# An attention and expert kernel on one core: more products of ones at the start, and two groups of loads issued by ScalarE

## The chip, the cores and the metric

The kernel runs on one core of one Trainium2 chip. The metric is the device time of the whole kernel in microseconds (us), the median of several executions. The engines are named as in the profile: PE (TensorE, products), PEld (its weight loads), DVE (VectorE), ACT (ScalarE), POOL (GpSimd) and SP (SyncE, which here only issues transfers). Each engine carries out its instructions in the order of its own queue; between engines they wait on semaphores. A transfer (DMA) is issued by SP or ACT, which each have a queue of their own (SPq, ACTq), and is carried out by 16 DMA engines; the issuing instruction itself takes time on the engine that issues it.

## The reference

Attention over two batches of eight heads, 576 positions of 64 values, in which each row keeps only its 32 largest scores; then a layer of four experts, weighted by probabilities that are divided by their sum.

```python
scores = scale * np.matmul(q, k.transpose(0, 1, 3, 2))
kth = np.partition(scores, -top_k, axis=-1)[..., -top_k:-top_k + 1]
scores = np.where(scores >= kth, scores, -1000000000.0)
attn = softmax(scores)                       # rows of 576
x = np.matmul(attn, v)                       # to (1152, 512)
p = domain_probs / (domain_probs.sum(-1, keepdims=True) + 1e-09)
for e in range(4):
    out += p[:, e:e + 1] * (np.maximum(x @ w1[e], 0.0) @ w2[e])
```

All inputs are 32-bit floats; w1 is 4 x 512 x 1024, w2 is 4 x 1024 x 512.

## The kernel before

The 1152 rows are cut into ten tiles: for each batch one of 64 rows and four of 128. The first tile worked on is the 64-row tile of batch 0. A tile is cut into units: a head for the tiles of 128 rows; for a tile of 64 rows a pair of heads, one in the upper and one in the lower half of the partitions. For each unit TensorE makes the scores, VectorE finds the 32 largest of each row (four times MAX8, line L666, with MATCH_REPLACE8, L668 and L670, between them), ScalarE takes the exponential, VectorE or ScalarE with GpSimd mask it (L717), and TensorE multiplies with the values. The expert layer of a tile (L894 to L896, L941) follows once its attention is done. 32-bit operands are split into a high and a low 16-bit part for this; only the first tile's attention works on 32-bit operands directly.

The order on every engine is written out by hand: pieces of work are given a place in one list (`at`, with the table `ISSUE`), and each engine's queue is filled in the order of that list. Code that stands outside `at` is put in where it stands, ahead of the list.

What happens at the start, and the names that matter:

- `kraw` holds the 576 keys of the eight heads of batch 0: `kraw0[:, 0:4, x, z, :]` the first 512 keys of head 4z+x, `kraw0[0:64, 4, ...]` the last 64 keys. `load_k0` (L1014 to L1016) issues two loads of 128 KB for one x; `load_k0_end` (L1022 to L1025) issues the two loads of the last 64 keys of all heads, 64 KB each.
- ACT issues `load_k0` for x = 0 and 2 (L1018, L1020). SP issues the queries of the first tile (`qraw`, two loads, L359), the last 64 keys, `load_k0` for x = 1 and 3, the queries of the second tile (`qraw`, L366), then four loads of the probabilities (`pn`, `norm_probs`, L1047 to L1050), and after those the first expert weights (`w`, L351) and the values (`vraw`, L334, L337).
- On TensorE a loop (L1039) multiplies a block of ones with itself into a bank that nobody reads. Then come the transposes of the first queries (L568, copied by ACT at L572), the transposes of the keys for x = 0 (L589, copied by ACT at L582 for the first 512 keys and at L583 for the last 64), and the scores of the first unit (L608, eight products). The first MAX8 (L666) reads these scores.
- `kv_gram` (L1070) sums squares over all of `kraw`; its diagonal goes to DVE at L1076 and a total back to it at L1079, L289.
- `norm_probs2` (L1053 to L1056) divides the probabilities by their sums on DVE; it is the first reader of the loaded `pn`. It stands in DVE's queue inside the first unit's search for maxima.
- ACT's table of functions is loaded (ACT_TABLE_LOAD) ahead of its first ACTIVATE (L1041), right behind ACT's own issues of loads. L382 squares the second tile's queries.

A queue of transfers uses eight semaphores in turn (`DMAHW0` to `DMAHW7` in the order below): an issue waits until the earlier transfer that raises the same semaphore has landed.

Of the kernel before, what the change touches and what calls it, by code (L numbers as in the profile page):

```python
# [229 lines left out]
def attn_moe_kernel(tc, q, k, v, probs, w1, w2, out):  # L230
    nc = tc.nc
    PE, ACT, DVE, POOL, SP = nc.tensor, nc.scalar, nc.vector, nc.gpsimd, nc.sync
# [38 lines left out]
    def at(place, fn, *args):  # L271

        i = len(known)
        known.append(fn.__name__)
        heapq.heappush(events, (ISSUE[i][0] if ISSUE else place, i, 0, fn, args))

    def bank(p, tag):
        return p.tile([128, 512], F32, tag=tag, name=tag)
# [17 lines left out]
    with tc.manual_schedule(engines={getattr(mybir.EngineType, x) for x in MANUAL}):  # L296
# [10 lines left out]
        pn = cp.tile([128, 10, E], F32, name="pn")  # L307
# [16 lines left out]
        kraw0 = scratch.tile([128, 5, 4, 2, D], F32, name="kraw0")  # L324
# [30 lines left out]
        def load_q(t, eng=SP):  # L355
            r = rawp.tile([128, 8, D], F32, tag="raw", name="qraw")
            if t == tiles[0]:
                for z in range(2):
                    eng.dma_start(out=r[0:64].rearrange("p (x z) d -> p x z d", z=2)[:, :, z, :],  # L359
                                  in_=q[t[0], 4 * z:4 * z + 4, t[1]:t[1] + 64, :].rearrange("h p d -> p h d"))  # L360
            elif t[2] == 64:
                for z in range(2):
                    eng.dma_start(out=r[z * 64:(z + 1) * 64, 0:4, :],
                                 in_=q[t[0], 4 * z:4 * z + 4, t[1]:t[1] + 64, :].rearrange("h p d -> p h d"))
            else:
                eng.dma_start(out=r, in_=q[t[0], :, t[1]:t[1] + 128, :].rearrange("h p d -> p h d"))  # L366
            qraw[t] = r
# [646 lines left out]
        def load_k0(eng, x):  # L1014
            for z in range(2):
                eng.dma_start(out=kraw0[:, 0:4, x, z, :], in_=k[0, 4 * z + x, 0:512, :].rearrange("(p j) d -> p j d", j=4))  # L1016

        load_k0(ACT, 0)  # L1018
        load_q(tiles[0])
        load_k0(ACT, 2)  # L1020

        def load_k0_end():  # L1022
            for z in range(2):
                SP.dma_start(out=kraw0[0:64, 4, :, z, :],
                             in_=k[0, 4 * z:4 * z + 4, 512:576, :].rearrange("h p d -> p h d"))  # L1025

        at(-200, load_k0_end)
        at(-199, load_k0, SP, 1)
        at(-198, load_k0, SP, 3)

# [5 lines left out]
        DVE.memset(ones, 1.0)  # L1036
        DVE.memset(kraw0[64:128, 4], 0.0)
        warm = bank(ps_m2, "m2")
        for _ in range(24):  # L1039
            PE.matmul(warm[:, 0:128], lhsT=ones.bitcast(BF16)[:, 0:128], rhs=ones.bitcast(BF16)[:, 0:128], start=True, stop=True)  # L1040
        ACT.activation(stp.tile([128, 1], F32, tag="warm", name="warm"), ones[:, 0:1], AF.Exp)  # L1041
        DVE.memset(pn, 1.0)
# [3 lines left out]

        def norm_probs():  # L1047
            for g, r0, n, m in ((0, 0, 128, 4), (4, 512, 64, 1), (5, S, 128, 4), (9, S + 512, 64, 1)):
                SP.dma_start(out=pn[0:n, g:g + m, :],
                             in_=probs[r0:r0 + n * m, :].rearrange("(t p) e -> p t e", p=n))  # L1050

        def norm_probs2():
# [73 lines left out]
        def norm_x0():  # L1126
            POOL.tensor_scalar(pn[:, 0:5], pn[:, 0:5], ix[:, 0:1], None, op0=OP.mult)

        at(P["probs"], norm_probs)
        at(P["probs2"], norm_probs2)  # L1130
        at(P["probs2"] + 1, norm_x0)
# [78 lines left out]
        for m, (e, j) in enumerate(worder):  # L1210
            for a in (0, 2):
                n = 4 * m + a
# [4 lines left out]
            g = P["gram"][m]  # L1217
            w_scale(e, j, g)
            g = max(P["split"][m], g + P["diag"], raw_used.get((e, j), 0) + 0.1)
# [5 lines left out]
        while events:  # L1225
            place, i, n, f, args = heapq.heappop(events)
# [38 lines left out]
```

## Time and profile before

| | us |
|---|---|
| median of 3 runs | 538.57 |
| lowest, highest run | 537.21, 541.6 |
| profiled execution | 536.48 |
| its span, from the first to the last instruction | 534.7 |
| mean granted TensorE clock | 0.979 of full |

How to read it: an engine's busy time is a mean over stages with different limits, so what matters is which engine the chain of work that ended last runs through at a given time. That chain is followed back from the last instruction; at each step it goes to whatever released the instruction, or to the one before it on its engine. "issue" is time in which nothing that the profile shows was waited for. The granted clock of TensorE has two levels here, 1.2 GHz (0.50 of full) and 2.4 GHz (1.00); a mean in between is a stretch that holds both. Before the first record the column shows 1.00.

### The profile page before, as it was taken

To read this page: it belongs to the slowest core of one execution; us is meant where nothing else is said; L and a number is where in the kernel's file an instruction comes from. 1 tells how busy PE (TensorE), PEld (TensorE's weight loads), DVE (VectorE), ACT (ScalarE), POOL (GpSimd) and SP (SyncE) were. 2 spreads that over 40 slices of the span, in tenths; PEclk is the share of its full clock that TensorE was granted. 3 is DMA by queue.
4 is the path that set the end of the run, shared out by engine and by line. 5 is a ranking of instruction groups with operands and counts; after the bars stand their busy time and mean duration, and the time that the engine had idled before them with its cause. 6 is when DMAs were issued, how large, how long until landed. Compare 5 with 4: busy or idle time off the path is not lost.

```text
span 534.7 us, 16328 instructions
## 1 busy us (share of the span) xinstructions
PE 502.9 (94%) x6738; PEld 382.4 (72%) x6738; DVE 433.2 (81%) x966; ACT 366.8 (69%) x610; POOL 361.1 (68%) x395
## 2 busy tenths in 40 slices
PE   7887677789999999999999999999999999999996
PEld 5566664676777777777877688678777876777766
DVE  3999999999999999999999998998889895500102
ACT  3999999998668788788768667676466664252112
POOL 0489999999776777786957867586556664434211
PEclk8998899899999999999999999999999999999999
DMA  7999999544743547384635642542532222302001
GB/s 172 350 328 296 268 252 220 107 71 86 104 83 75 101 86 128 95 145 84 134 78 97 120 90 66 73 79 47 75 72 54 51 56 50 60 22 46 12 2 32
DMA packets 142780, 58.37 MB, mean 109 GB/s; under 512 B 130097, under 2 KB 134449, under 8 KB 142705
## 3 DMA queue, kind: packets, MB, share of 16 engines
q1 hardware_dynamic: 139280, 54.50, 48.7%
q10 hardware_dynamic: 3424, 2.82, 1.7%
q8 instruction: 53, 0.87, 0.7%
q14 instruction: 23, 0.18, 0.1%
HBM read 25.45 MB, written 2.36 MB: 52 GB/s over the span
## 4 chain that ended last, share of the span: by engine, by line
PE 78%; DVE 17%; ACT 2%; issue 1%; DMA 1%; SPq 0%; DVEq 0%; ACTq 0%
PE m L941 33%; PE m L894 11%; PE m L896 11%; PE m L895 11%; DVE m L666 7%; PE av L777 5%; PE ps L653 5%; DVE w L670 4%; DVE w L668 2%; DVE w L717 2%; DMA kraw<-in_k_dram 1%; PE m L952 1%; ACT w L542 1%; PE av L952 0%; PE ps L649 0%
## 5 line engine op out<-in xcount | busy, mean ns | idle before, releaser
L896 PE MATMUL m<-xt,w 128*128 128x128 f16 (+1 forms) x1280 | 199.8, 215 | 1.4 <-POOL w L545 1.4
L941 PE MATMUL m<-w,h 128*128 128x512 f16 (+1 forms) x912 | 191.8, 383 | 0.0
L894 PE MATMUL m<-xt,w 128*128 128x128 f16 (+1 forms) x1120 | 179.1, 215 | 0.0
L895 PE MATMUL m<-xt,w 128*128 128x128 f16 (+1 forms) x1120 | 179.0, 215 | 0.0
L666 DVE MAX8 m<-w 128x8 f32<-128x576 f32 x216 | 161.6, 755 | 3.0
L941 PEld LDWEIGHTS <-h 128*128 128x128 f16 (+1 forms) x912 | 81.7, 101 | 89.0 <-issue 3.1
L896 PEld LDWEIGHTS <-w 128*128 128x128 f16 x1280 | 124.1, 99 | 1.5 <-POOL w L545 1.5
L894 PEld LDWEIGHTS <-w 128*128 128x128 f16 x1120 | 108.9, 99 | 3.0 <-issue 1.0
L895 PEld LDWEIGHTS <-w 128*128 128x128 f16 x1120 | 108.6, 99 | 1.9
L670 DVE MATCH_REPLACE8 w<-m,w 128x576 f32<-128x576 f32 x144 | 106.9, 742 | 0.0
L919 POOL TENSOR_TENSOR h<-hf,h 128x512 f16<-128x512 f32 x56 | 64.9, 1158 | 56.1 <-ACT hf L912 48.7
L738 POOL TENSOR_TENSOR a<-w,a 128x512 f16<-128x512 f32 x68 | 78.8, 1160 | 22.7 <-ACT a L736 13.0
L727 POOL TENSOR_TENSOR w<-w,d 128x576 f32<-128x576 f32 x49 | 62.7, 1280 | 37.0 <-ACT d L724 36.8
L710 ACT ACTIVATE w<-ps,nb,es 128x576 f32<-128x576 f32 x68 | 56.2, 827 | 42.9 <-DVE m L666 35.1
L905 ACT ACTIVATE h<-m 128x512 f16<-128x512 f32 x72 | 42.5, 590 | 57.2 <-PE m L896 39.3
L666 DVE MAX8 m<-ps 128x8 f32<-128x576 f32 x72 | 54.4, 756 | 19.6 <-PE ps L608 7.1
L988 DVE SCALAR_TENSOR_TENSOR o<-m,pniw,o 128x512 f32<-128x512 f32 (+1 forms) x13 | 9.7, 746 | 56.2 <-PE m L941 46.7
L736 ACT ACTIVATE a<-w 128x576 f16<-128x576 f32 x68 | 45.9, 679 | 11.8 <-POOL w L727 9.3
L668 DVE MATCH_REPLACE8 w<-m,ps 128x576 f32<-128x576 f32 x72 | 53.8, 747 | 0.0
L653 PE MATMUL ps<-kt,qa 128*128 128x288 f16 x128 | 34.3, 288 | 14.5 <-DVE w L717 13.7
L777 PEld LDWEIGHTS <-at 128*128 128x128 f16 (+1 forms) x1008 | 37.0, 100 | 7.5 <-DMA at<-a 2.2
L777 PE MATMUL av<-vt,at 128*128 128x65 f16 (+1 forms) x1008 | 40.1, 195 | 1.3 <-DMA at<-a 1.3
(163 smaller groups left out, 784.0 us busy)
## 6 DMA issues: line engine op xcount, KB each, us to landing
w<-in_moe_w_dram SPq DMA_DIRECT2D x16, 1024.0 KB, 7.2
qraw<-in_q_dram SPq DMA_DIRECT2D x8, 256.0 KB, 3.5
qb<-qa SPq DMA_DIRECT2D x16, 128.0 KB, 2.6
out_dram<-o ACTq DMA_DIRECT2D x8, 256.0 KB, 2.0
at<-a SPq DMA_TRANSPOSE x68, 3.3
vraw<-in_v_dram SPq DMA_DIRECT2D x2, 512.0 KB, 9.1
nraw<-in_v_dram SPq DMA_DIRECT2D x4, 256.0 KB, 3.4
kraw<-in_k_dram SPq DMA_DIRECT2D x4, 256.0 KB, 3.3
```

What stands on the lines that cost most here:

```text
L653: PE.matmul(ps[:, 0:288], lhsT=src[:, x, :], rhs=kt[x].rearrange("p c n -> p (c n)")[:, ks], start=(j == 0), stop=(j == 1))
L666: DVE.max(m, s_t[u] if r == 0 else w_t[u])
L668: DVE.match_replace(rows2(w_t[u]), m, s_t[u], NEG)
L670: DVE.match_replace(w_t[u], m, w_t[u], NEG)
L727: POOL.tensor_tensor(w, w, g, op=OP.mult)
L738: POOL.tensor_tensor(a[:, 640:1152], w[:, 0:512], a[:, 0:512], op=OP.subtract)
L777: PE.matmul(o, lhsT=att[:, blk, ps], rhs=r, start=(i == 0), stop=(i == len(seq) - 1))
L894: PE.matmul(o, lhsT=HI[e, 0, c][:, fc], rhs=xs(0, c), start=(c == 0), stop=False)
L895: PE.matmul(o, lhsT=HI[e, 0, c][:, fc], rhs=xs(1, c), start=False, stop=False)
L896: PE.matmul(o, lhsT=LO[e, 0, c][:, fc], rhs=xs(0, c), start=False, stop=(c == 3))
L919: POOL.tensor_tensor(h[:, 1], hf, h[:, 0], op=OP.subtract)
L941: PE.matmul(y[z * 64:z * 64 + M, :], lhsT=h_t[es, qd][:, p // 2, h0:h0 + M], rhs=w, start=(fc == 0 and p == 0), stop=(fc == 7 and p == 2))
```

## The change

Three edits at the start of the program; nothing else is changed, and the order of the instructions on DVE and POOL is the same.

1. The loop over products of ones runs 36 times instead of 24.
2. The two loads of the last 64 keys are split up: the one for heads 4 to 7 (z = 1) is issued by ACT, between `load_k0` for x = 0 and for x = 2; the one for heads 0 to 3 (z = 0) stays on SP.
3. The four loads of the probabilities are issued by ACT instead of SP.

```diff
+        def load_k0_end(eng, z):
+            eng.dma_start(out=kraw0[0:64, 4, :, z, :],
+                          in_=k[0, 4 * z:4 * z + 4, 512:576, :].rearrange("h p d -> p h d"))
+
         load_k0(ACT, 0)
         load_q(tiles[0])
+        load_k0_end(ACT, 1)
         load_k0(ACT, 2)
-
-        def load_k0_end():
-            for z in range(2):
-                SP.dma_start(out=kraw0[0:64, 4, :, z, :],
-                             in_=k[0, 4 * z:4 * z + 4, 512:576, :].rearrange("h p d -> p h d"))
-
-        at(-200, load_k0_end)
+        at(-200, load_k0_end, SP, 0)
         at(-199, load_k0, SP, 1)
         at(-198, load_k0, SP, 3)
...
-        for _ in range(24):
+        for _ in range(36):
             PE.matmul(warm[:, 0:128], lhsT=ones.bitcast(BF16)[:, 0:128], rhs=ones.bitcast(BF16)[:, 0:128], start=True, stop=True)
...
-                SP.dma_start(out=pn[0:n, g:g + m, :],
+                ACT.dma_start(out=pn[0:n, g:g + m, :],
                              in_=probs[r0:r0 + n * m, :].rearrange("(t p) e -> p t e", p=n))
```

SP's queue at the start of the program, before the change. The names are destination and source of each load; behind them stands the semaphore that the issue waits for.

```order
L359 DMA qraw<-in_q_dram 64x4x64 x2
L1024 DMA kraw_143<-in_k_dram 64x4x64 x2
L1016 DMA kraw_143<-in_k_dram 128x4x64 [waits DMAHW0_49]
L1016 DMA kraw_143<-in_k_dram 128x4x64 [waits DMAHW1_49]
L1016 DMA kraw_143<-in_k_dram 128x4x64 [waits DMAHW2_49]
L1016 DMA kraw_143<-in_k_dram 128x4x64 [waits DMAHW3_49]
L366 DMA qraw<-in_q_dram 128x8x64 [waits DMAHW4_49]
L1049 DMA pn<-in_moe_domain_probs_dram 128x4x4 [waits DMAHW5_49,DVE_49]
L1049 DMA pn<-in_moe_domain_probs_dram 64x4 [waits DMAHW6_49]
L1049 DMA pn<-in_moe_domain_probs_dram 128x4x4 [waits DMAHW7_49]
L1049 DMA pn<-in_moe_domain_probs_dram 64x4 [waits DMAHW0_49]
L351 DMA w_123<-in_moe_w_dram 128x2x1024 [waits DMAHW1_49]
```

The same place on SP after the change:

```order
L359 DMA qraw<-in_q_dram 64x4x64 x2
L1019 DMA kraw_143<-in_k_dram 64x4x64
L1016 DMA kraw_143<-in_k_dram 128x4x64
L1016 DMA kraw_143<-in_k_dram 128x4x64 [waits DMAHW1_49]
L1016 DMA kraw_143<-in_k_dram 128x4x64 [waits DMAHW2_49]
L1016 DMA kraw_143<-in_k_dram 128x4x64 [waits DMAHW3_49]
L366 DMA qraw<-in_q_dram 128x8x64 [waits DMAHW4_49]
L351 DMA w_123<-in_moe_w_dram 128x2x1024 [waits DMAHW5_49]
```

One load of the last keys and the four loads of the probabilities are gone from SP, and the first expert weights stand directly behind the second tile's queries.

ACT's queue at the start of the program, before the change (m is the bank that TensorE writes, kf and qf are the copies of its transposes):

```order
L1016 DMA kraw_143<-in_k_dram 128x4x64 x4
L1041 ACT_TABLE_LOAD
L1041 ACTIVATE warm<-ones 128x1 [waits DVE_49]
L572 ACTIVATE qf<-m_195 128x256 [waits PE_49]
L582 ACTIVATE kf<-m_204 128x512 [waits PE_49]
L583 ACTIVATE kf<-m_205 128x64 [waits PE_49]
L382 ACTIVATE qhl,qss<-qraw 128x512 [waits DMAHW4_49]
```

The same place on ACT after the change (line numbers behind L1016 are one lower in the changed program, and buffers are numbered anew):

```order
L1016 DMA kraw_143<-in_k_dram 128x4x64 x2
L1019 DMA kraw_143<-in_k_dram 64x4x64
L1016 DMA kraw_143<-in_k_dram 128x4x64
L1016 DMA kraw_143<-in_k_dram 128x4x64 [waits DMAHW0_49]
L1040 ACT_TABLE_LOAD
L1040 ACTIVATE warm<-ones 128x1 [waits DVE_49]
L572 ACTIVATE qf<-m_208 128x256 [waits PE_49]
L582 ACTIVATE kf<-m_216 128x512 [waits PE_49]
L583 ACTIVATE kf<-m_217 128x64 [waits PE_49]
L1048 DMA pn<-in_moe_domain_probs_dram 128x4x4 [waits DMAHW6_49,DVE_49]
L1048 DMA pn<-in_moe_domain_probs_dram 64x4 [waits DMAHW7_49]
L382 ACTIVATE qhl,qss<-qraw 128x512 [waits DMAHW4_49]
```

(Two more loads of the probabilities stand between the last two rows, for batch 1.) The issue of the last keys stands third, ahead of the keys for x = 2, whose second load now waits for a semaphore; the probabilities stand between the copy of the last keys and the square of the second tile's queries.

## Rows read from the trace of the kernel before

**Rows 1.** The page: the span, and the chain that ended last by engine.

```profile
span 534.7 us, 16328 instructions
PE 78%; DVE 17%; ACT 2%; issue 1%; DMA 1%; SPq 0%; DVEq 0%; ACTq 0%
```

**Rows 2.** Stretches: length, busy of PE, PEld, DVE, ACT, POOL; clock; DMA share; GB/s.

```profile
25.00:30.00 5.00, 4.05 (x48) 3.02 (x48) 4.93 (x13) 5.00 (x6) 3.87 (x4) 1.00 1.20 299
```

**Rows 3.** The chain in order of time, 0 to 60 us: start, length, what.

```profile
3.08 3.49 DMA kraw<-in_k_dram
...
8.92 0.78 DVE m L666
```

**Rows 4.** The chain in order of time, 60 to 125 us.

```profile
85.12 0.66 ACT a L736
...
94.61 0.82 DVE w L717
```

**Rows 5.** The timeline, 0 to 34 us: start, length, engine, line, what [idle before].

```profile
0.73 2.72 ACTq L1016 DMA_DIRECT2D kraw<-in_k_dram  x4
...
1.04 2.74 PE L1040 MATMUL m<-ones 128*128 128x128 bf16 x24 [1.04 <-DVE ones L1036]
...
3.48 1.28 ACT L1041 ACT_TABLE_LOAD   x1 [3.48 <-issue]
...
4.78 0.20 ACT L1041 ACTIVATE warm<-ones 128x1 f32<-128x1 f32 x1
...
5.25 0.43 PE L568 MATMUL m<-ident,qraw 64*128 64x64 f32 x4 [1.47 <-DMA qraw<-in_q_dram]
...
5.71 0.38 ACT L572 ACTIVATE qf<-m 128x256 f32<-128x256 f32 x1 [0.73 <-PE m L568]
6.30 0.60 ACT L582 ACTIVATE kf<-m 128x512 f32<-128x512 f32 x1 [0.20 <-PE m L589]
6.60 0.62 SPq L366 DMA_DIRECT2D qraw<-in_q_dram  x1
...
6.71 0.24 PE L589 MATMUL m<-ident,kraw 64*128 64x64 f32 x1 [0.45 <-DMA kraw<-in_k_dram]
...
6.95 1.93 PE L608 MATMUL ps<-kf,qf 64*64 64x288 f32 x8
6.99 0.22 ACT L583 ACTIVATE kf<-m 128x64 f32<-128x64 f32 x1
7.35 2.35 SPq L1049 DMA_DIRECT2D pn<-in_moe_domain_probs_dram  x4
...
9.74 1.10 SPq L351 DMA_DIRECT2D w<-in_moe_w_dram  x2
...
10.15 0.63 ACT L382 ACTIVATE qhl<-qraw 128x512 bf16<-128x512 f32 x1 [2.94 <-DMA qraw<-in_q_dram]
...
12.26 0.19 DVE L1053 TENSOR_REDUCE psumr<-pn 128x10 f32<-128x40 f32 x1
...
13.54 1.19 PE L608 MATMUL ps<-kf,qf 64*64 64x288 f32 x8
...
17.25 1.09 PE L507 MATMUL m<-w 128*128 128x128 bf16 x16 [0.70 <-DMA w<-in_moe_w_dram]
```

**Rows 6.** Stretches of 1 us, columns as in the second group.

```profile
7.00:8.00 1.00, 1.00 (x6) 0.59 (x8) 0.00 (x0) 0.21 (x1) 0.00 (x0) 0.63 0.63 142
...
10.00:11.00 1.00, 0.99 (x11) 0.81 (x9) 0.97 (x2) 0.81 (x3) 0.00 (x0) 0.67 0.33 23
...
13.00:14.00 1.00, 0.98 (x8) 0.55 (x8) 1.00 (x7) 1.00 (x3) 0.00 (x0) 1.00 1.00 410
```

**Rows 7.** DMA issues, 0 to 1 us: count, KB each, median us to landing.

```profile
kraw<-in_k_dram ACTq DMA_DIRECT2D x1, 128.0 KB, 2.7
```

**Rows 8.** The four loads of pn, 0 to 20 us, from issue to landing.

```profile
DMA to landing us min/median/max: 1.9/2.3/3.0
```

**Rows 9.** DMA issues, 0 to 20 us, columns as in the seventh group.

```profile
vraw<-in_v_dram SPq DMA_DIRECT2D x4, 64.0 KB, 8.2
```

## The prediction, made before the changed kernel ran

> **What bounds the kernel now.** First the page: of the chain of work that ended last, 78% is TensorE and 17% VectorE [rows 1]. The products of the expert layers fill the engine later on; the question is what this change, which touches only the first twenty microseconds, does to the moment at which they can run. So I read the chain in order of time. It begins with a load: the second load of the last 64 keys travels from 3.08 to 6.57 us, the transpose that needs it ends at 6.95, eight score products (L608) follow, and VectorE's first search for maxima (L666) starts at 8.92 [rows 3, 5]. From there VectorE is the chain: it is busy 4.93 of 5 us between 25 and 30 [rows 2], and the chain leaves it only at 85.12 us, for ScalarE, and comes back to it at 94.61 [rows 4]. A microsecond won ahead of 8.92 is therefore won for a VectorE that never rests afterwards; a microsecond lost on VectorE between 8.92 and 85 is lost in the same way.
>
> Next the timeline of the start. The 24 products of ones run from 1.04 to 3.78, 0.114 us apart; a product of the same shape at 17.25 stands 0.068 apart (16 in 1.09) [rows 5], where the granted clock is full. TensorE then idles 1.47 us until the queries land at 5.25. The score products of the first unit take 1.93 us, those of the second unit, eight of the same shape at 13.54, 1.19 us [rows 5]. The granted clock explains it: it fell in the slice from 7 to 8 us (mean 0.63, so about 0.74 us of the slice at half, 1.2 GHz), and was back at 2.4 GHz in the slice from 13 to 14 [rows 6]. What TensorE did before it fell: that idle stretch of 1.47 us, the first transposes, another 0.45 us of waiting for the last keys.
>
> **The change, part by part.** The sum is made against the profiled execution, 536.48 us (span 534.7); the median of the runs shown, 538.57, is 2.09 above it.
>
> *Twelve more products of ones.* At 0.114 us each they would run from 3.78 to 5.15, at 0.068 to 4.60. Either way they end ahead of 5.25, where the queries land [rows 5], so they cost nothing themselves: the idle 1.47 us covers them, and without that cover they would cost 0.82 to 1.37 us. The pause shrinks to between 0.10 and 0.65 us. What they can give is the clock: at full speed the first unit's score products take 1.19 instead of 1.93, that is −0.74 us. Bounds: 0 if the clock falls all the same, −0.74 if it holds. I take −0.74, since the idle stretch ahead of the fall is cut by more than half and the second one goes too (next part).
>
> *One load of the last keys goes to ScalarE's queue, third there.* Four issues there take 2.72 us, 0.68 each [rows 5], so it is issued at 2.09; with the 3.49 us that the same load takes today [rows 3] it lands at 5.58 instead of 6.57. The other stands on SyncE where the first of the two stands today, so it lands no later than now. The last transposes (L589) then run at about 6.3. But the score products also need the copy L582, which runs on ScalarE from 6.30 to 6.90 [rows 5] and does not depend on these keys. So the products can start at 6.90 rather than 6.95: −0.05, and no more, although the load that the chain names is almost a microsecond earlier.
>
> *What this pushes back on ScalarE.* Five issues instead of four: the table load starts at 4.16 instead of 3.48, takes 1.28, the first ACTIVATE 0.20, so ScalarE is free at 5.66; the copy of the queries starts at 5.71 [rows 5]. Covered by the 0.73 us for which ScalarE waits there today, with 0.05 left. The order shows that the last of the five now waits for the semaphore that the first key load raises; that load lands after 2.7 us [rows 7], at 3.43, and the issue's turn comes at 3.45. Cost 0. If it took 3.49 us like the other one, the issue, table load and copy would be 0.77 late, less 0.05 here and some 0.2 ahead of L582: 0.5 us lost. I take 0.
>
> *The loads of the probabilities leave SyncE.* SyncE issues these four from 7.35 to 9.70 and the first two expert weights at 9.74 [rows 5]. The weights move up behind the loads of the keys and queries, whose last issue ends at 7.22, to about 7.3: 2.4 us earlier. Nobody on VectorE waits for them: the one product that does, at 17.25, idles 0.70 us [rows 5] on a TensorE that has time there. Gain 0; bounds 0 and −0.7.
>
> *They arrive on ScalarE*, behind the copy of the last keys (L583, end 7.2), and hold it for the same 2.35 us, to about 9.55. Behind them in its queue stands the square of the next queries (L382), which today waits 2.94 us for its own load and starts at 10.15 [rows 5]: covered. The reader of the probabilities is VectorE, at L1053, 12.26 us. With VectorE 0.79 us ahead it comes there at 11.47. At 0.59 us an issue the last one starts at 8.96; at the 1.9 to 3.0 us that these loads take now [rows 8] it lands between 10.9 and 12.0, and at 11.3 with the median of 2.3: no stall. But they now travel beside the weights. The nearest row for a small load among large ones is that of the last values, 64 KB, 8.2 us to landing [rows 9]: that would be 17.2 and a stall of 5.7 us. Between 0 and 5.7 I take 0, because those value loads stood behind 2 MB and more in their own queue, while ScalarE's queue is empty when the probabilities come.
>
> **Sum:** −0.74 − 0.05 = −0.79 us; 536.48 becomes 535.7, and in terms of the median 537.8. VectorE's order and everything behind is the same, so I carry the shift through whole; ScalarE's stretch from 85.12 to 94.61 on the chain could swallow it, which is a reason not to go lower.
>
> **Rivals.**
>
> *The probabilities come late (slower).* Mechanism: the weights' two loads, 2048 KB, lie on the same 16 DMA engines from about 10.1 us on (the next queries land ahead of them), and at the 410 GB/s of the slice from 13 to 14 [rows 6] they need 5.0 us, to 15.1. The last two loads of probabilities are 576 rows of 16 bytes, 36 for each engine, against 32 weight rows of 4 KB for each engine; if the engines take turns between the two queues, the probabilities are through when the weights are. VectorE then stands at L1053 from 11.47 to 15.1, 3.6 us, and the result is 537.8 + 3.6 = 541.4; at the 8.2 us bound 543.5. It decides against the change from the point at which L1053 starts later than 12.26. For it: VectorE is in order, only 0.2 us of slack is left at the median landing, and the stretch that the probabilities have to themselves today, at 23 GB/s between 10 and 11 us [rows 6], is then full of weights. Against it: nothing in this trace shows a load on one queue held up by the other. The Trainium skill, DMA: Bandwidth & Descriptors, section "Queues, rings and completion order", says that each DMA engine goes round the queues that have work and changes only after a whole packet; by that rule this rival is what happens, near 541.4 by the terms above. The trace has no stretch in which small rows on ScalarE's queue meet large rows on SyncE's, so it neither bears the rule out nor refutes it.
>
> *The clock falls anyway (no change).* If the clock rises while the extra products run, they are done at 4.60 and a pause of 0.65 us stays, then about 0.4 us ahead of the score products. Then only −0.05 is left: 538.5. For it: the stretch with the fall holds two pauses, and only one fall ahead of 20 us is there to judge by. Against it: TensorE also pauses for 0.70 us ahead of 17.25 [rows 5], a pause like the one that would be left, and the products behind it run at full speed, 0.068 us apart.
>
> *Earlier weights help more than I say:* the weights of the first expert, 2.4 us earlier, shorten a later wait: 536 or less. The chain shows no such wait, so this stays small.
>
> **How the numbers follow.** Forecast (clock holds, probabilities in time) 0.45, its own range 536.3 to 539.3; probabilities late 0.32, 538.8 to 543.5; clock falls anyway 0.20, 537.5 to 539.5; more than that 0.03. The runs shown lie between 537.21 and 541.6, so the median itself may move by a microsecond or two. 535.5 to 542.5 leaves out the upper part of the late case and little else. One per cent, about what a measurement of this kernel can tell from no change, is 5.4 us. The forecast moves 0.8, the slow rival at its bound 5.0: faster by over 1% 0.02, within 1% 0.94, slower by over 1% 0.04.
>
> **What would show it.** Right: products of ones up to 4.6 or 5.15; granted clock 1.00 in the slice from 7 to 8 us; eight score products in about 1.2 us from 6.9; the first L666 near 8.15; L1053 near 11.5 without idle time before it; the chain leaving VectorE for ScalarE at about 84.3. Wrong: a first L666 still at 8.9 (the clock); idle time on VectorE ahead of L1053, ended by the load of pn, and a time to landing of those loads well over 3 us (the slow rival); a copy L572 later than 5.71 (ScalarE's issues). If L666 starts early and the time does not follow, the shift was swallowed between 85 and 95 us.

## The result: 1.0% slower, and the profile after

The changed kernel takes 543.98 us (median of 4 runs, 542.91 to 545.36). The kernel before takes 537.89 beside it (median of 4 runs, 536.55 to 541.60). The ratio is 1.010, with a 95% interval of 1.0063 to 1.0136. I had predicted 537.8 with a range of 535.5 to 542.5: the time lies above the range, and what happened is the first rival, at a higher price than I gave it.

Line numbers behind L1016 are one lower in the changed kernel: the products of ones are L1039, the loads of the probabilities L1048, their first reader L1052.

The page of the profile after: the span, and the chain that ended last by engine.

```profile
span 541.2 us, 16350 instructions
PE 79%; DVE 7%; issue 6%; DMA 3%; POOL 2%; ACT 2%; POOLq 0%; SPq 0%
```

The profiled execution took 543.11 us against 536.48 before, 6.63 more. Against [rows 1] VectorE has fallen from 17% of the chain to 7%, and 6% is now "issue". That looks as if VectorE mattered less. It doesn't; I come back to it below.

The timeline of the start: start, length, engine, line, what, and in brackets the idle time before it and what ended it.

```profile
1.04 3.68 PE L1039 MATMUL m<-ones 128*128 128x128 bf16 x36 [1.04 <-DVE ones L1035]
...
5.14 0.43 PE L568 MATMUL m<-ident,qraw 64*128 64x64 f32 x4 [0.41 <-DMA qraw<-in_q_dram]
5.61 0.38 ACT L572 ACTIVATE qf<-m 128x256 f32<-128x256 f32 x1
...
6.84 1.19 PE L608 MATMUL ps<-kf,qf 64*64 64x288 f32 x8 [0.48 <-ACT kf L582]
...
6.98 2.55 ACTq L1048 DMA_DIRECT2D pn<-in_moe_domain_probs_dram  x4
...
7.17 1.61 SPq L351 DMA_DIRECT2D w<-in_moe_w_dram  x2
...
8.08 0.77 DVE L666 MAX8 m<-ps 128x8 f32<-128x576 f32 x1 [6.28 <-PE ps L608]
...
17.66 0.19 DVE L1052 TENSOR_REDUCE psumr<-pn 128x10 f32<-128x40 f32 x1 [6.17 <-DMA pn<-in_moe_domain_probs_dram]
```

Read against [rows 5]: the ones end at 4.72 and leave a pause of 0.41 us instead of 1.47; the copy of the queries is not late; the score products of the first unit take 1.19 us instead of 1.93; the first search for maxima starts at 8.08 instead of 8.92. Up to here the change has won 0.84 us. Then VectorE stands still for 6.17 us in front of the sums of the probabilities, which start at 17.66 instead of 12.26.

The waits of the first 30 us: who waited for whom, us in total, times, longest.

```profile
POOL qhl L397 <- ACT qhl L392: 24.1, 1, 24.1
...
ACT kraw L1112 <- DVE k0ps L291: 6.2, 1, 6.2
...
DVE psumr L1052 <- DMA pn<-in_moe_domain_probs_dram: 6.2, 1, 6.2
```

These three rows explain the chain of the page. The sums stand in VectorE's queue ahead of L291; ScalarE waits 6.2 us for L291 with the scaling of the keys (L1112), and GpSimd waits behind ScalarE until 25.6. The chain that ended last goes back through GpSimd this time, and books the long wait, which the waits put down to ScalarE, as "issue":

```profile
1.58 24.02 issue
```

Beside it stands VectorE's stop, which the waits show and the chain does not name.

Stretches of 1 us: length, busy of PE, PEld, DVE, ACT, POOL; clock; DMA share; GB/s.

```profile
7.00:8.00 1.00, 1.00 (x9) 0.36 (x8) 0.00 (x0) 0.00 (x0) 0.00 (x0) 1.00 1.03 232
10.00:11.00 1.00, 0.36 (x5) 0.19 (x3) 1.00 (x5) 0.81 (x3) 0.00 (x0) 1.00 1.00 353
15.00:16.00 1.00, 0.00 (x0) 0.00 (x0) 0.00 (x0) 0.00 (x0) 0.00 (x0) 1.00 1.06 363
```

The stretch from 10 to 11 us, in which the DMA engines moved 23 GB/s in [rows 6] because little more than the probabilities was under way, is now full of weights at 353 GB/s. From 15 to 16 no compute engine does anything; the DMA engines are full.

The four loads of the probabilities, from issue to landing, where [rows 8] had 1.9/2.3/3.0:

```profile
DMA to landing us min/median/max: 6.8/8.0/9.2
```

And the DMA queues, packets, MB and share of 16 engines, from 10 to 12 us and then from 12 to 13 (q1 is SyncE's queue, q10 ScalarE's):

```profile
q1 hardware_dynamic: 179, 0.73, 98.3%
q10 hardware_dynamic: 45, 0.00, 1.2%
...
q1 hardware_dynamic: 91, 0.32, 78.1%
q10 hardware_dynamic: 318, 0.00, 17.7%
```

For 2 us ScalarE's queue moved 45 small packets while SyncE's moved 179 large ones; in the next microsecond it moved 318. The last of the four loads had been issued by 9.53 (four issues, 2.55 us from 6.98 on), so I read these numbers as small rows that stood ready and did not get their turn; the profile shows issue and landing, not readiness.

### The profile page after: what moved, and what is told of

Read it like the earlier page. It is cut to its first block, busy times and chain, and to the rows that moved or that the text cites. A ratio compares the mean times of both kernels' runs of the same rounds, so it can differ in the third digit from the quotient of the medians.

```text
span 541.2 us, 16350 instructions
## 1 busy us (share of the span) xinstructions
PE 506.2 (94%) x6750; PEld 385.9 (71%) x6750; DVE 433.4 (80%) x966; ACT 367.4 (68%) x610; POOL 361.3 (67%) x395
## 3 DMA queue, kind: packets, MB, share of 16 engines
HBM read 25.45 MB, written 2.36 MB: 51 GB/s over the span
## 4 chain that ended last, share of the span: by engine, by line
PE 79%; DVE 7%; issue 6%; DMA 3%; POOL 2%; ACT 2%; POOLq 0%; SPq 0%
PE m L941 33%; PE m L894 11%; PE m L896 11%; PE m L895 11%; PE av L777 5%; PE ps L653 5%; DVE m L666 3%; DMA at<-a 2%; DVE w L670 2%; DMA qb<-qa 1%; DVE w L668 1%; DVE w L717 1%; POOL w L545 1%; POOL khl L1099 1%; ACT w L536 1%
## 5 line engine op out<-in xcount | busy, mean ns | idle before, releaser
L777 PEld LDWEIGHTS <-at 128*128 128x128 f16 (+1 forms) x1008 | 37.1, 100 | 9.8 <-DMA at<-a 4.6
L777 PE MATMUL av<-vt,at 128*128 128x65 f16 (+1 forms) x1008 | 40.2, 195 | 3.7 <-DMA at<-a 3.6
```

Of the source, the lines that this page charges most:

```text
L777: PE.matmul(o, lhsT=att[:, blk, ps], rhs=r, start=(i == 0), stop=(i == len(seq) - 1))
```

## The experiments

The theory after this result: the third edit alone costs the time, because small rows on ScalarE's queue wait behind weights that SyncE now issues at the same moment, and VectorE takes the sums in order. The rivals: the loss comes from the loads of the last keys or from ScalarE's issues; the probabilities are late for a reason of ScalarE's queue itself; or the first two edits cost something that the profile hides.

### Which edit costs the time

The third edit alone, put into the kernel before:

```diff
-                SP.dma_start(out=pn[0:n, g:g + m, :],
+                ACT.dma_start(out=pn[0:n, g:g + m, :],
```

> The kernel before with one edit alone: ScalarE issues the probabilities. If the wait for them is the whole loss of the change: pn lands at 17 to 18 us, VectorE waits at L1053, the first L666 stays near 8.9, and the time is 6 to 7 us above before (544 to 546). If the loss needs the other two edits as well: within 2 us of before.

Measured: 544.20 us (median of 5 runs) against 539.04 (24 runs), ratio 1.0082, interval 1.0055 to 1.0110. The timeline, and the time to landing of the four loads:

```profile
8.38 0.77 DVE L666 MAX8 m<-ps 128x8 f32<-128x576 f32 x1 [6.58 <-PE ps L608]
...
18.60 0.19 DVE L1053 TENSOR_REDUCE psumr<-pn 128x10 f32<-128x40 f32 x1 [6.18 <-DMA pn<-in_moe_domain_probs_dram]
```

```profile
DMA to landing us min/median/max: 7.8/8.9/10.1
```

The same wait, 6.18 us, and within the noise the same time as the whole change: this edit is enough for the loss. (The first search starts at 8.38 and not near 8.9, because the score products took 1.48 us in this execution.)

The opposite, the whole change without its third edit (36 products of ones and the split keys stay):

```diff
-                ACT.dma_start(out=pn[0:n, g:g + m, :],
+                SP.dma_start(out=pn[0:n, g:g + m, :],
```

> The change with one edit undone: the probabilities are issued by SyncE again; 36 products of ones and the split loads of the last keys stay. If the late probabilities are the whole loss: L1052 starts near 11.5 us with no idle time before it, first L666 near 8.1, and 0.8 us less than before (537.1 against 537.9). If the products of ones or the split keys cost something later on (an earlier VectorE meets transfers that are not ready): between 538.5 and 544.

Measured: 541.28 (10 runs) against 539.02 (19 runs), 1.0027, interval 1.0003 to 1.0051. Its timeline:

```profile
11.46 0.19 DVE L1052 TENSOR_REDUCE psumr<-pn 128x10 f32<-128x40 f32 x1
...
19.05 1.89 PE L507 MATMUL m<-w 128*128 128x128 bf16 x16 [3.19 <-DMA w<-in_moe_w_dram]
...
20.98 0.30 DVE L513 SCALAR_TENSOR_TENSOR m<-m,ident 128x128 f32<-128x128 f32 x1 [2.36 <-PE m L507]
```

The wait for the probabilities is gone, and the sums start 0.80 us earlier than in [rows 5]. But the kernel does not get faster: it is 0.3% slower than before, just clear of the noise, and the profiled execution (539.12 us) is one of the faster of its ten. So the first two edits together do not bring the 0.79 us of the sum; the split keys were not run alone. The second half of the products that square the weights (L507) now idles 3.19 us for the second load of weights, and VectorE, which takes their diagonal at L513, idles 2.36 us behind them. So a new wait stands a few microseconds behind the old one.

The first edit alone, in the kernel before:

```diff
-        for _ in range(24):
+        for _ in range(36):
```

> The kernel before with 36 products of ones and nothing else. If the held clock is worth what it saves in the first scores: 0.7 us less than before (538.3 against 539.0), L666 near 8.2. If the second load of the weights, which is read at L507 and L513, sets the pace right behind: no difference from before, and VectorE waits ahead of L513 by what it won. If the clock rises and falls at other times in each execution, whatever the number of products: no difference from before, and L608 takes 1.2 or 1.9 to 2.2 us by chance.

Measured: 539.72 (10 runs) against 539.04 (24 runs), 1.0008, interval 0.9984 to 1.0032: no change that can be told, though the interval, from −0.9 to +1.7 us, still has room for the 0.74 that I expected. Its timeline:

```profile
6.91 1.19 PE L608 MATMUL ps<-kf,qf 64*64 64x288 f32 x8
...
18.42 1.34 PE L507 MATMUL m<-w 128*128 128x128 bf16 x16 [2.66 <-DMA w<-in_moe_w_dram]
...
87.12 0.16 DVE L797 TENSOR_SCALAR r<-av 128x4 f32<-128x4 f32 x1 [1.48 <-PE av L777]
```

The score products take 1.19 us, as the first step of my sum said, but in this execution nothing of it is left further on: VectorE loses 1.16 us at L513 behind the late weights, 0.9 at L289, and 1.48 at L797 behind the products with the values (L777), which wait for a transposed load. The weights were issued at 9.52 us here and at 9.74 in [rows 5], yet the second half of the products idles 2.66 us here and 0.70 there. What differs is the landing: the second load of weights lands at 18.38 here (8.2 us after its issue) and at 19.00 in the version above (8.8), against 17.20 in the profile before (6.8). In that profile L513 stands here:

```profile
19.33 0.29 DVE L513 SCALAR_TENSOR_TENSOR m<-m,ident 128x128 f32<-128x128 f32 x1
```

The products that it reads end at 18.34, 0.99 us earlier. With the load landed at 17.20, a VectorE that is 0.79 us ahead would not have had to wait; the wait comes from the later landing. Why the load landed later in these two profiles they don't show.

### Is it the wait alone?

The change as it is, but with the sums of the probabilities moved back in VectorE's order, from inside the first unit to the third (entry 29 of the table ISSUE, the place of `norm_probs2`):

```diff
-C_QK, C_V0, C_W1, C_W2 = 11, 14, 6, 14
+C_QK, C_V0, C_W1, C_W2 = 11, 14, 6, 14; ISSUE[29] = (78.5,)
```

> The change as it is, but the four small operations on the probabilities (norm_probs2) stand later in VectorE's queue, behind the diagonal of the values near 24 us; the loads themselves are issued by ScalarE and travel as in the change. If only VectorE's wait for them costs: they still land near 17.6 us, nobody waits, and 0.8 us less than before (537.1). If the weights that now travel 2.4 us earlier, or the late loads themselves, disturb anything else: 539 to 544 without a wait at L1052.

Measured: 539.87 (10 runs) against 539.02 (19 runs), 1.0007, interval 0.9986 to 1.0028. The timeline, and the time to landing of the probabilities:

```profile
5.44 0.66 PE L568 MATMUL m<-ident,qraw 64*128 64x64 f32 x4 [0.38 <-DMA qraw<-in_q_dram]
...
7.83 2.18 PE L608 MATMUL ps<-kf,qf 64*64 64x288 f32 x8 [0.39 <-ACT kf L582]
...
26.89 0.19 DVE L1052 TENSOR_REDUCE psumr<-pn 128x10 f32<-128x40 f32 x1
```

```profile
DMA to landing us min/median/max: 5.9/7.5/9.4
```

The loads are as late as in the changed kernel, up to 9.4 us; nobody waits for them, and the loss against the kernel before is gone. The 537.1 that I expected it does not reach: the 0.8 us of the first two edits is missing here as it is with the probabilities back on SyncE. So late probabilities cost nothing in themselves that can be told: the price is VectorE's in-order wait. The same profile shows, in passing, that 36 ones don't always bring the short score products: they took 2.18 us here.

### Why the loads are late

The values ahead of the weights on SyncE (entries 3 and 4 of ISSUE, the first two loads of weights, go behind the values), all else as changed:

```diff
-C_QK, C_V0, C_W1, C_W2 = 11, 14, 6, 14
+C_QK, C_V0, C_W1, C_W2 = 11, 14, 6, 14; ISSUE[3], ISSUE[4] = (36.2,), (36.4,)
```

> The change, but SyncE issues the two loads of the values ahead of the first two loads of the weights, so that the probabilities meet rows of 1 KB and 256 bytes first instead of rows of 4 KB. If the DMA engines take turns row by row between the two queues: 36 turns of 0.046 us instead of 0.159, about 1.7 us, so the last load of pn lands near 12 and L1052 starts at 12 to 12.5; time 538 to 539 unless the late weights cost. If the loads wait until the bytes issued around them have gone by: 1.3 MB of values at 400 GB/s, 3.2 us, and then weights: L1052 at 15 to 18, time 541 to 544.

Measured: 544.36 (one run) against 539.02. The timeline, and the landing of the probabilities:

```profile
13.51 0.20 DVE L1052 TENSOR_REDUCE psumr<-pn 128x10 f32<-128x40 f32 x1 [1.34 <-DMA pn<-in_moe_domain_probs_dram]
...
21.28 1.89 PE L507 MATMUL m<-w 128*128 128x128 bf16 x16 [4.42 <-DMA w<-in_moe_w_dram]
```

```profile
DMA to landing us min/median/max: 4.3/4.7/4.9
```

With the values beside them, whose rows are 1 KB (four neighbouring rows of 64 values of 32 bits) and, for the last 64 positions, 256 bytes, in place of weight rows of 4 KB, the probabilities land after at most 4.9 us instead of 9.2, on the same queue of ScalarE. So what SyncE moves beside them decides in this one run, not ScalarE's queue itself. The sums start at 13.51, later than by turns of one row (12 to 12.5 expected) and earlier than after all the bytes issued around them (15 to 18). The time stays bad, now beside late weights: 4.42 us of waiting at L507, and 5.03 us for VectorE behind it at L513.

Fewer, longer rows for the probabilities, 64 bytes instead of 16 in the two loads of 512 rows, where a partition takes four neighbouring rows; the two loads of 64 rows stay as they are (this gives the tiles of 128 rows the probabilities of other rows, a change in what is computed):

```diff
-                             in_=probs[r0:r0 + n * m, :].rearrange("(t p) e -> p t e", p=n))
+                             in_=probs[r0:r0 + n * m, :].rearrange("(p t) e -> p t e", p=n))
```

> The change, with the same 18 KB of probabilities loaded in fewer rows: four neighbouring rows of the input go to one partition (so the 128-row tiles get the probabilities of other rows; that part of the computation is changed). 384 rows instead of 1152, 24 instead of 72 for each DMA engine. If turns by row decide: the last two loads need 12 turns instead of 36, about 1.9 us beside the weights, L1052 near 12 to 13, time near 538.5. If it is the bytes ahead of them, or a fixed delay of a load on ScalarE's queue beside the weights: L1052 still near 17.6, time 543 to 544.

Measured: 541.93 (one run) against 539.02. The timeline, the landing, and the DMA queues from 10 to 11.5 us:

```profile
14.95 0.20 DVE L1052 TENSOR_REDUCE psumr<-pn 128x10 f32<-128x40 f32 x1 [3.49 <-DMA pn<-in_moe_domain_probs_dram]
```

```profile
DMA to landing us min/median/max: 3.3/6.0/6.4
```

```profile
q1 hardware_dynamic: 133, 0.54, 99.6%
q10 hardware_dynamic: 7, 0.00, 0.3%
```

A third of the rows brings the wait from 6.17 to 3.49 us (one run): the number of rows counts. But from 10 to 11.5 us only 7 packets of ScalarE's queue moved, and 133 of SyncE's. If each engine took one row of either queue in turn, the two numbers would be about equal, and the second load of probabilities, 64 rows or four for each engine, would be held up by four large rows, 0.7 us at the 0.18 us that one takes (99.6% of 16 engines' 1.5 us, over 133). It landed 5.8 us after its issue, at 13.07, while the first, ahead of it in the queue, had landed at 10.23. So the turns are not of one row each.

How large is a turn? The same 2 MB of weights as one load (of 32 rows of 4 KB for each engine), and as four loads, instead of two, the rest as changed:

```diff
+            if (e, j) == (0, 0):
+                if a == 2:
+                    return
+                b = 4
```

> The change, but the first 2 MB of weights are one load instead of two of 1 MB (32 rows of 4 KB for each DMA engine in one piece; the three loads of probabilities issued after it meet one load instead of two). If an engine serves the two queues load by load: hardly any row of pn moves until the 2 MB are through, that is from 10 to 14.5 us, and all later loads of pn land after 15. If an engine changes queues after a run of rows that is shorter than 32: rows of pn move near 12 to 13 as in the change. If it changes after each row: they move evenly from 9.5 on. L1052 near 17 to 18 in all three; the packets of queue q10 between 10 and 14.5 us tell them apart.

```diff
+            if (e, j) == (0, 0) and b - a == 2:
+                for c in (a, a + 1):
+                    load_w(eng, e, j, c, c + 1)
+                return
```

> The change, but the first 2 MB of weights are four loads of 512 KB, eight rows for each engine. If a turn of the weights' queue ends with the load or with a run of rows cut at the load's end: turns of 1.3 us instead of 2.5, the first loads of pn land near 11 to 12 instead of 13.8 and 14.7, L1052 at 13 to 16. If a turn is a run of rows that goes on over the end of a load, or if the bytes issued ahead decide: no difference, L1052 near 17.5.

Measured: 544.15 with one load, 542.38 with four (one run each) against 539.16. The sums (L1056 here) and the landing, with one load:

```profile
19.05 0.20 DVE L1056 TENSOR_REDUCE psumr<-pn 128x10 f32<-128x40 f32 x1 [6.91 <-DMA pn<-in_moe_domain_probs_dram]
```

```profile
DMA to landing us min/median/max: 8.7/9.6/10.4
```

With four loads:

```profile
15.59 0.20 DVE L1056 TENSOR_REDUCE psumr<-pn 128x10 f32<-128x40 f32 x1 [3.89 <-DMA pn<-in_moe_domain_probs_dram]
```

```profile
DMA to landing us min/median/max: 2.9/5.2/7.0
```

The wait goes with the size of the load beside it: 3.89 us at 512 KB, 6.17 at 1 MB, 6.91 at 2 MB, at the same bytes of weights in all. That would fit turns that end with a load or a piece of one, but does not show them. Between 1 and 2 MB the step is small beside the scatter: the slowest of the four loads landed after 9.2, 9.4 and 10.1 us in the three profiles with loads of 1 MB (the change, the sums moved back, the third edit alone), and after 10.4 with 2 MB. With four loads the probabilities were issued 0.26 us earlier (6.72), and their first two loads had landed, after 2.9 and 3.4 us, before any load of weights had. And SyncE issued the last two of the four loads of weights only at 9.19 and 10.79 us, and the first values at 13.21 instead of 8.91, so less was issued ahead of the probabilities too: the rival that the bytes ahead decide is not excluded. Nor did ScalarE's queue stand still until a whole load of 2 MB was through: with one load, 77 of its packets moved from 12 to 13 us beside 101 of SyncE's. How many rows one turn holds stays open.

### Other places for the four loads

On SyncE, but behind the first weights and values, with the sums in the third unit:

```diff
-C_QK, C_V0, C_W1, C_W2 = 11, 14, 6, 14
+C_QK, C_V0, C_W1, C_W2 = 11, 14, 6, 14; ISSUE[28], ISSUE[29] = (59.5,), (78.5,)
...
-                ACT.dma_start(out=pn[0:n, g:g + m, :],
+                SP.dma_start(out=pn[0:n, g:g + m, :],
```

> 36 products of ones and the split keys as in the change; the probabilities are issued by SyncE, behind the first weights and values, and their sums (norm_probs2) stand later on VectorE, behind the diagonal of the values. The weights come 2.4 us earlier without small rows beside them. If the second load of the weights held back what the first edits won: L507 no longer waits, VectorE 0.8 us ahead through L513, 537.5 to 538.3. If earlier weights and an earlier start are worth nothing: 539 to 541 as with the probabilities on SyncE.

Measured: 539.14 (10 runs) against 539.04 (24 runs), 1.0002, interval 0.9986 to 1.0017. The timeline, and a wait of VectorE:

```profile
16.84 1.09 PE L507 MATMUL m<-w 128*128 128x128 bf16 x16 [1.05 <-DMA w<-in_moe_w_dram]
```

```profile
DVE r L797 <- PE av L777: 1.6, 1, 1.6
```

The first search for maxima starts at 8.17, the weights are issued at 7.15, and VectorE waits neither for probabilities nor at L513 here, though L507 still idles 1.05 us. At 21 us it is 2.35 us ahead of the profile before, though part of that is the sums that it does later: at 24.6, with the sums done, it is level. At L797 (84 us before) the products with the values are late, and it is 1.69 us behind.

Issued by GpSimd at the very start, right behind its first memsets (entry 28 of ISSUE is the place of `norm_probs`), the rest as changed:

```diff
-C_QK, C_V0, C_W1, C_W2 = 11, 14, 6, 14
+C_QK, C_V0, C_W1, C_W2 = 11, 14, 6, 14; ISSUE[28] = (-1,)
...
-                ACT.dma_start(out=pn[0:n, g:g + m, :],
+                POOL.dma_start(out=pn[0:n, g:g + m, :],
```

> The change with the probabilities issued by GpSimd, at about 1.6 us, where GpSimd idles until 20 us; ScalarE and SyncE are both rid of them, and the weights travel 2.4 us earlier as in the change. If the loss came from small rows that meet the weights: they land before 9 us, no wait at L1052, 0.8 us less than before or better, since the weights come earlier too (537 to 538.3). If 1152 rows of 16 bytes hold up the first keys and queries: the first L666 0.5 to 1 us later than in the change, time near 539.

Measured: 537.01 (8 runs) against 539.04 (24 runs), 0.9969, interval 0.9940 to 0.9999. Its timeline:

```profile
2.11 2.87 POOL L1048 DMA_DIRECT2D pn<-in_moe_domain_probs_dram  x4 [0.53 <-DVE pn L1041]
...
7.24 1.31 SPq L351 DMA_DIRECT2D w<-in_moe_w_dram  x2
...
11.63 0.19 DVE L1052 TENSOR_REDUCE psumr<-pn 128x10 f32<-128x40 f32 x1
...
13.87 2.18 PE L608 MATMUL ps<-kf,qf 64*64 64x288 f32 x8
...
16.10 0.77 DVE L666 MAX8 m<-ps 128x8 f32<-128x576 f32 x1 [1.08 <-PE ps L608]
...
17.32 2.39 PE L507 MATMUL m<-w 128*128 128x128 bf16 x32
```

The probabilities are issued from 2.11 us on and land within 4.0, before the weights exist on the DMA engines. In this execution both waits are gone: the sums start at 11.63 with no idle time, and L507 runs through its 32 products without one. But the weights did not come earlier for that. Their second load, issued at 8.07 instead of 10.37, landed after 9.1 us at 17.13, against 17.20 in the profile before; TensorE came to it later, at 17.32, after a stretch from 12 to 18 us with a granted clock of 0.50. In that stretch VectorE waits 1.08 us for the score products of 13.87, and the 0.63 us by which it was ahead are gone. The same kernel once more, in more runs:

> The version with the probabilities on GpSimd, 36 products of ones and the split keys once more, in more rounds: 0.3% under before if the first measurement was no chance (537 against 539), within 0.15% of before if it was.

Measured: 537.01 (12 runs) against 539.16 (23 runs), 0.9964, interval 0.9936 to 0.9992. It is the one version that beats both kernels, by intervals that twice leave out 1.000, if narrowly: about 2 us under the kernel before, 7 under the changed one. In its second profile, of 537.87 us, the probabilities land in 3.2 to 4.2 us and nobody waits for them, but L507 idles 1.28 us for the second weights again.

And the loads on GpSimd alone, put into the kernel before (24 ones, both key loads on SyncE), by the same entry of ISSUE and POOL in place of SP:

> The kernel before with one edit: GpSimd issues the probabilities at the start; 24 products of ones, both loads of the last keys on SyncE. If the gain of 2 us with GpSimd issuing them beside the other edits comes from SyncE's free queue and the earlier weights: the same here, 0.3% under before. If it needs the earlier first scores as well: no difference from before.

Measured: 538.95 (10 runs) against 539.16 (23 runs), 0.9991, interval 0.9969 to 1.0012. Weights that are issued 2.4 us earlier are worth nothing there that can be told; nor did they land earlier, the second load at 17.37 us against 17.20. Its timeline has the first search for maxima at 9.19 us, behind score products of 2.11:

```profile
9.19 0.77 DVE L666 MAX8 m<-ps 128x8 f32<-128x576 f32 x1 [7.39 <-PE ps L608]
```

So neither the ones alone (539.72) nor the free SyncE queue alone (538.95) brings what both together with the split keys bring (537.01). One might think of two waits in a row, of which each edit removes one: early scores are held up by late weights, early weights wait for late scores. The runs don't bear that out. The weights that were issued early landed hardly earlier than in the profile before (16.80 to 17.37 against 17.20), and the version with the probabilities behind the values had early scores and an early issue of the weights too and stayed at 539.14. The winner's first profile (536.76 us) does not lie ahead of the profile before on VectorE at 95 us, it is 0.47 us behind; and that one execution of before, 536.48 us, was faster than all other runs of the same kernel on record (536.55 and more), so it is a poor yardstick for half a microsecond. Where the 2 us come from stays open.

One thing all 13 profiles with edits share. Take the distance of VectorE to the profile before at one instruction, the MATCH_REPLACE8 that starts at 96.86 us there: it is the difference of the whole execution to within 0.2 us. It is 6.57 us where the time differs by 6.63 in the changed kernel, 8.01 and 7.98 with the third edit alone, 3.31 and 3.31 with 36 ones alone, 2.60 and 2.62 with the probabilities behind the values, 0.47 and 0.28 in the winner's first profile. So what VectorE has lost or won by then goes whole into the time, and it is lost at few places. In the changed kernel 5.40 of the 6.57 us stand at the sums, and most of the rest comes at L797 (84 us before), where VectorE waits 1.22 us for the products with the values; the profile before has no such wait.

## Why the prediction was wrong

**Twelve more ones, −0.74: right in size at the first scores; nothing of it seen in the time.** In the changed kernel the score products took 1.19 us, VectorE started 0.84 us earlier, and I had said 0.79. But I carried the shift through whole, with "VectorE's order and everything behind is the same". The order is the same, and a shift that VectorE still has at 97 us does go whole into the time; what the instructions wait for until then is not the same. Alone, the edit left the time at 1.0008 of before, with an interval too wide to rule the 0.74 out: in its profile VectorE ran into the second load of weights (L513, 1.16 us) and the products with the values (L797, 1.48 us). I had given the wait of 0.70 us ahead of 17.25 to "a TensorE that has time there" and "Nobody on VectorE waits for them". VectorE does, one step further, at L513. It had 0.99 us of slack there in the profile before, more than the shift; the wait came up because the second load landed 1.2 us later than there, and 1.8 us later with the probabilities back on SyncE.

**The last keys, −0.05, and ScalarE's issues, 0: right.** The copy of the queries started at 5.61, before the 5.71 of [rows 5], and the products were released by the copy L582, as I had said.

**The probabilities, "between 0 and 5.7 I take 0": this step failed.** Measured: 6.17 us of wait, more than even the upper bound. The reason that I gave for the lower end, that ScalarE's queue is empty when the probabilities come, looked at the wrong resource. The queue was empty, the 16 engines behind it were not: from 10 to 12 us they served 179 large packets of SyncE's and 45 small ones of ScalarE's. The nearest row that I had, 8.2 us for the small values [rows 9], was the better guide, although those stood in their own queue; measured were 6.8 to 9.2. With this one term, 537.8 + 6.2 = 544.0, and the measurement is 543.98. That the two agree so closely is luck. The sum starts from 538.57, and the kernel before took 537.89 beside the changed one; its −0.79 did not show in the time when the probabilities were back on SyncE (541.28 against 539.02); and of the 6.6 us that the profile lost, 1.2 came behind the sums.

**The rival "the probabilities come late": the mechanism right, the price not.** I had let the probabilities be through when the 2 MB of weights are, at 15.1, for 3.6 us. The last of them landed at 17.59, and the second load of weights itself only at 16.27. The values follow the weights on SyncE's queue at once, and the rows of the probabilities moved in bursts: 474 packets from 9 to 10 us, 45 from 10 to 12, 318 from 12 to 13. In the prediction I set this rule of the Trainium skill (DMA: Bandwidth & Descriptors, section "Queues, rings and completion order") against the absence of a row: an engine goes round its queues and changes only after a whole packet of descriptors. The traces agree with it so far that, with loads of both queues outstanding, the engines did not change after each row (179 packets against 45 from 10 to 12 us); how long a turn is and what ends it none of these runs shows. I gave the rival 0.32 where the forecast had 0.45. The two facts that I had already written for it, 0.2 us of slack and a stretch at 23 GB/s that would fill with weights, deserved the larger share.

**Earlier weights, 0: not contradicted, but for another reason.** I had taken weights that are issued 2.4 us earlier for weights that arrive earlier; my rival had them through at 15.1. Issued early, their second load landed at 17.13, 17.30, 17.37 and 16.80 in the four profiles with the probabilities on GpSimd or behind the values, against 17.20 in the profile before. Only beside the two profiles with 36 ones and a late issue (18.38 and 19.00) is that earlier. With 24 ones and the keys as before, the early issue left the time at 0.9991 of before.

**The clock falls anyway: not here, but the step was less certain than I wrote.** Over the profiles with 36 ones the first score products took 1.19 us in all but one, 2.18 there; with 24 ones 1.93, 1.48 and 2.11. The slices of the granted clock don't tell this: before the first record the column shows 1.00, and it does so from 7 to 8 us in the execution with 2.18 as well. The duration of the products is the reading to trust.

## What to carry to other kernels

Moving small loads to an idle queue is not free when the move lets large loads start at the same moment: look at what the DMA engines will be carrying when the small rows arrive, and at how much slack the first reader has, here 0.2 us on an engine that takes its work in order. Small loads that are read early should be issued before the large ones exist, or their reader should stand later in its engine's order. A lead won at the start of a saturated engine is a gain only if no wait behind it takes it back; here it was lost within 20 us, once to a load that landed later and once to products at the half clock. And an earlier issue is not yet an earlier landing: read the landing.

## What the runs showed of the hardware

- The four loads of probabilities, 1152 rows of 16 bytes in all, took 1.9 to 3.3 us each to land when SyncE issued them ahead of the weights, 6.8 to 9.2 (7.8 to 10.1 with the third edit alone, 5.9 to 9.4 with the sums moved back) on ScalarE's queue beside loads of 1 MB on SyncE's, 4.3 to 4.9 on the same queue beside the values, and 3.0 to 4.2 from GpSimd ahead of the weights.
- The second of the two loads of weights landed after 6.8 us in the profile before (the two have a median of 5.9 and the first took 5.0), and after 8.2 and 8.8 with 36 ones alone and with the probabilities back on SyncE, though it was issued within 0.3 us of the same time. A wait of 0.70 us in one profile became 2.66 and 3.19. Issued near 8 us instead of 10.37, it landed between 16.80 and 17.37 in four profiles, hardly earlier than the 17.20 of the profile before.
- TensorE's granted clock fell to half in later places when the start was kept at full. In the fastest kernel it was 0.50 from 12 to 18 us, behind a slice (10 to 11 us) in which TensorE was busy for 0.36 us, and the score products at 13.87 took 2.18 us. In the kernel with the probabilities on SyncE it was 0.50 from 19 to 22 us, behind the idle stretch of 3.19 us, and the score products at 20.87 took 1.93. What the products of ones save at the start can be paid again later.
